# Two decode layers on one core: layer 0's output product runs one pair behind, its last two output weights load last, the MLP loads are recut, and the tile context is dropped

## The chip, the cores and the metric

The kernel runs on one core of one Trainium2 chip. The metric is the device time of one execution in microseconds (us). Six runs of the kernel before gave 523.41 to 524.87 us, with a median of 523.86 us.

## The reference

One token goes through two layers that share all their weights. Each layer is attention over a sliding window followed by a gated MLP, both with a residual:

```python
x = x + A(layernorm(x)); x = x + B(layernorm(x))      # twice, same weights and caches
# A: 32 heads of 192, the last 4096 keys and values of each head
q = (x @ wq).reshape(B, Sq, 32, 192)
p = softmax(einsum("bhqd,bhkd->bhqk", q, k) * 192**-0.5)
o = einsum("bhqk,bhkd->bhqd", p, v);  A = o.reshape(B, Sq, 32*192) @ wo
# B: 640 -> 1536 -> 640
h = sigmoid(x @ w_gate) * (x @ w_up);  B = h @ w_down
```

All is bf16. x has 640 elements. There is one query, so every weight and every cache entry is used once per layer, and 219 MB come from HBM in an execution.

## The kernel before, in words

**Units and slots.** The 32 heads are worked in 16 pairs. For each pair the host has laid out two units of 128 partitions by 14208 elements (3552 KB, KB of 1024 bytes): `ua[p]` holds the query weights (1920 elements) and then the keys, `ub[p]` holds the values (VE = 12288 elements, head after head) and then the output weights (WOE = 1920 elements). SBUF has seven slots of one unit (L132) and a region `mreg` of 12288 elements, which is 19.2 cells of FW = 640. The MLP's gate, up and down weights are 12 cells each. `A_SLOT` and `B_SLOT` (L183 to L189) say which slot a unit goes to. In layer 0 the ua units alternate between slots 0 and 1 and the ub units between slots 2 and 3, apart from a few. Units a0, a1, a14, a15, b0, b14 and b15 stay in their slots after layer 0 and are used again in layer 1 without a load (`KEPT`); in layer 1 the values of pair 1 (PM) go into `mreg`, and its output weights ("wom") into the slot of a1 once that pair's query product is done.

**Loads.** All loads are issued from SyncE (L182) in the fixed order of the list `seq` (L204 to L209): a0, a1, b0, a2, b1, a3, b2, ... a15, b14, then pair 15's second-head values with its output weights ("b1"), its first-head values in two halves ("b0"), and then the layer-0 MLP: gate cells 0 to 4 and 5 to 11 ("wg"), up cells 0 to 6 ("u1") and 7 to 11 ("u2"), down cells 0 to 6 ("d1") and 7 to 11 ("d2"), the values of pair PM in three parts ("va", "vb", "vc"). Then come layer 1's a2 in two parts ("a0"), "wom", and the pairs up to 13, and the weights of the last MLP. A load is planned as soon as the list reaches it and its place is free: `release` frees a slot, `mark` records an event, and `try_load` (L222) refuses an item whose event is not there yet. On the chip SyncE waits in this order for the semaphore of the reader that frees the place. "u2" waits for the first gate product, "d1" for both, "d2" for the first part of the up product, and "va" to "vc" for both down products.

**A step.** `step(p, prev)` (L459) computes the query product Q(p) on TensorE (L351), the scores QK(p) (L366), the maximum in `soft` (VectorE L376, ScalarE L379, TensorE L382, VectorE L383 and L385), the exponential (ScalarE L390), then for the pair before the product with the values PVmm (L420) and its copies (ScalarE L425), for p the transposed probabilities ET (L396, L400, L403, L405), and at last PVout of the pair before: six small matmuls (L435), one VectorE multiply into `oTb` (L438) and 15 matmuls with the output weights into `yT` (L445). The last of these frees the ub slot. Layer 0 runs pair 0 by hand, `step(1, 0)`, and a loop on TensorE over the steps 2 to 15, then PVmm and PVout of pair 15 and the residual (L334). Layer 1 begins with the kept pairs 14, 15, PM and 0 in an interleaved order written out by hand, and then runs the same steps.

**MLP of layer 0.** Sum, centring, the gate product in two parts and the up product in two parts (`proj`, L558), the sigmoid as Exp, add and reciprocal (L588 to L590), the product `hT` in two parts (L593), the down product in two parts (L605), the residual.

**Ends.** The kernel opens a tile context (L795) with one critical section (L113). `finish` (L610) follows the block: the last down product per load (L617), a copy (L621), the store (L623), a wait for it, and six semaphore clears (L626).

Of the kernel before, what the change touches and what calls it, by code (L numbers as in the profile page):

```python
# [44 lines left out]
class _Prog:  # L45

    def __init__(self):
        self.ops = {e: [] for e in ("pe", "dve", "act", "dma", "adma")}
        self.cnt = {e: 0 for e in ("pe", "dve", "act")}
        self.dcnt = {}  # L50
        self.seg = None
# [55 lines left out]
def decode_kernel(ctx: ExitStack, tc: tile.TileContext, cx: bass.AP, ua: bass.AP, ub: bass.AP,  # L107
                  wg_d: bass.AP, wu_d: bass.AP, wd_d: bass.AP, out: bass.AP):
    nc = tc.nc
# [3 lines left out]
    ctx.enter_context(tc.tile_critical(name="decode", no_gpsimd_drain=True))  # L113
# [24 lines left out]
    sh = sb("sh", [P, 6 * DC + 4 + FC], BF16)  # L138
# [3 lines left out]
    oTb = sh[:, 6 * DC:6 * DC + 3]  # L142
    hT = sh[:, 6 * DC + 4:6 * DC + 4 + FC]
# [26 lines left out]
    rm = {n: res("m_" + n) for n in "abc"}  # L170
    MOFF = {"a": (0, 5 * FW), "b": (5 * FW, 12 * FW), "c": (12 * FW, ME)}
# [32 lines left out]
    seq += [("wg", 0), ("wg", 1), ("u1",), ("u2",), ("d1",), ("d2",), ("va",), ("vb",), ("vc",)]  # L204
    tail = stream(1, range(2, 14))
    assert tail[0] == ("a", 1, 2)
    seq += [("a0", 0), ("a0", 1), ("wom",)] + tail[1:]
    seq += [("fg",), ("fu",), ("fd", 0), ("fd", 1), ("fd", 2)]
    seq_pos = [0]  # L209
    busy = set()  # L210
# [3 lines left out]
    GH = 5  # L214
# [10 lines left out]
    def try_load(it):  # L225
        k = it[0]
        if k in ("a", "b"):
            s = (A_SLOT if k == "a" else B_SLOT)[it[1]][it[2]]
            if not take(s):
                return False  # L230
            pg.dma(q_dma(slot(s, 0, UNIT), (ua if k == "a" else ub)[it[2]]), f"s{s}", wr=[rslot[s]])
        elif k == "b1":
            s = B_SLOT[it[1]][it[2]]
            if not take(s):
                return False
            n = len(pg.ops["dma"])
            pg.dma(q_dma(slot(s, NB * DH, UNIT - NB * DH), ub[it[2]][:, NB * DH:]), f"s{s}", wr=[rslot[s]])
            ev_done["b1"] = list(pg.ops["dma"][n]["deps"].items())
        elif k == "b0":
            s = B_SLOT[it[1]][it[2]]  # L240
            o = it[3] * NHALF
            pg.dma(q_dma(slot(s, o, NHALF), ub[it[2]][:, o:o + NHALF]), f"bh{it[3]}", wr=[res(f"bh{it[3]}")], extra=ev_done["b1"])
        elif k == "a0":
            if f"a14_{it[1]}" not in ev_done:
                return False
            s = A_SLOT[1][2]
            o0, o1 = ((0, A0CUT), (A0CUT, UNIT))[it[1]]
            pg.dma(q_dma(slot(s, o0, o1 - o0), ua[2][:, o0:o1]), f"a0{it[1]}", wr=[res(f"a0{it[1]}")] + ([rslot[s]] if it[1] else []),
                   extra=[ev_done[f"a14_{it[1]}"]])
        elif k == "wg":  # L250
            f0, f1 = ((0, GH), (GH, FC))[it[1]]
            pg.dma(q_dma(mreg(f0 * FW, (f1 - f0) * FW), wg_d[:, f0 * FW:f1 * FW]), f"wg{it[1]}", wr=[[rm["a"]], [rm["b"]]][it[1]])
        elif k == "u1":
            pg.dma(q_dma(mreg(12 * FW, 7 * FW), wu_d[:, 0:7 * FW]), "u1", wr=[rm["c"]])
        elif k == "u2":
            if "gate0" not in ev_done:
                return False
            pg.dma(q_dma(mreg(0, 5 * FW), wu_d[:, 7 * FW:]), "u2", wr=[rm["a"]])
        elif k == "d1":
            if "gate1" not in ev_done:  # L260
                return False
            pg.dma(q_dma(mreg(5 * FW, 7 * FW), wdp(0, 7)), "d1", wr=[rm["b"]], extra=[ev_done["gate0"]])
        elif k == "d2":
            if "up0" not in ev_done:
                return False
            pg.dma(q_dma(mreg(12 * FW, 5 * FW), wdp(7, 12)), "d2", wr=[rm["c"]])
        elif k in ("va", "vb", "vc"):
            if "down0" not in ev_done:
                return False
            o0, o1 = MOFF[k[1]]  # L270
            pg.dma(q_dma(mreg(o0, o1 - o0), ub[PM][:, o0:o1]), k, wr=[rm[k[1]]])
        elif k == "wom":
            if "QM" not in ev_done:
                return False
            pg.dma(q_dma(slot(A_SLOT[1][PM], 0, WOE), ub[PM][:, VE:UNIT]), "wom", wr=[res("wom")], extra=[ev_done["QM"]])
        elif k == "fg":
            pg.dma(q_dma(mreg(0, 12 * FW), wg_d), "fg", wr=[rm["a"], rm["b"], rm["c"]])
        elif k == "fu":
            if not take(U_SLOT):
                return False  # L280
            pg.dma(q_dma(slot(U_SLOT, 0, 12 * FW), wu_d), f"s{U_SLOT}", wr=[rslot[U_SLOT]])
        else:
            if it[1] == 0 and not take(D_SLOT):
                return False
            c0, c1 = WFIN[it[1]]
            pg.dma(q_dma(slot(D_SLOT, c0 * D, (c1 - c0) * D), wdp(c0, c1)), f"wf{it[1]}", wr=[rslot[D_SLOT]] if it[1] == 0 else [])
        return True
# [50 lines left out]
    def attention(l, xi):  # L338
# [6 lines left out]
        def Q(p, y):  # L345
            sa = A_SLOT[l][p]

            def f(t):
                for i, c0 in enumerate((0, P, 2 * P)):
                    for c in range(DC):  # L350
                        ins = t.matmul(qe[:, i:i + 1], lhsT=slot(sa, c * 2 * DH + c0, P), rhs=xq[:, c:c + 1], start=(c == 0), stop=(c == DC - 1))  # L351
                return ins
            ev = pg.op("pe", f, rd=[res("xq"), rslot[sa]] + ([res("a00")] if l == 1 and p == 2 else []), ex=[rb[3]])
            pg.op("dve", lambda v: v.tensor_tensor(out=qs[:, y], in0=qe[:, 0:3].unsqueeze(2).to_broadcast([P, 3, 32]), in1=mask3, op=ALU.mult),  # L354
                  rd=[res("cst")], wr=[res(f"qs{y}")], ex=[rb[3]])
            return ev
# [51 lines left out]
        def PVmm(p, z):  # L408
# [3 lines left out]
            for h in (1, 0) if half else (0, 1):  # L412
                vt = (mreg(h * NB * DH, NB * DH) if inm else slot(sv, h * NB * DH, NB * DH)).rearrange("p (t d) -> p t d", t=NB)
                for part in (0, 1) if half and h == 0 else (None,):
# [8 lines left out]
                    rV = list(rm.values()) if inm else [rslot[sv]] + ([] if part is None else [res(f"bh{part}")])  # L423
# [4 lines left out]
        def PVout(p, z):  # L428
            inm = l == 1 and p == PM
            sv = None if inm else B_SLOT[l][p]  # L430

            def tm(t):
                for c in range(3):
                    for sg in range(2):
                        ins = t.matmul(oT3[:, c:c + 1], lhsT=o8_sb[:, sg, c:2 * DH:3], rhs=mask2[:, sg:sg + 1], start=(sg == 0), stop=(sg == 1))  # L435
                return ins
            pg.op("pe", tm, rd=[res("o8sb0"), res("o8sb1"), res("cst")], ex=[rb[6]])
            pg.op("dve", lambda v: v.tensor_scalar(out=oTb, in0=oT3[:, 0:3], scalar1=Rn[z], scalar2=None, op0=ALU.mult),  # L438
                  rd=[res(f"Rn{z}0"), res(f"Rn{z}1")], wr=[res("oTb")], ex=[rb[6]])
            wo = slot(A_SLOT[1][PM], 0, WOE) if inm else slot(sv, VE, WOE)  # L440

            def im(t):
                for j in range(DC):
                    for c in range(3):
                        ins = t.matmul(yT[:, j:j + 1], lhsT=wo[:, c * D + j * P:c * D + (j + 1) * P], rhs=oTb[:, c:c + 1],  # L445
# [3 lines left out]
            pg.op("pe", im, rd=[res("oTb")] + ([res("wom"), rslot[sa]] if inm else [rslot[sv]]), ex=[rb[7]])  # L449
            if inm:  # L450
                release(sa)
            elif not (l == 0 and ("b", p) in KEPT):
                release(sv)

# [4 lines left out]
        def step(p, prev):  # L459
            Q(p, 0)  # L460
            QK(p, 0)
            soft()
            expo()
            PVmm(prev, prev % 2)
            ET(p % 2)
            PVout(prev, prev % 2)
# [14 lines left out]
        if l == 0:  # L481
# [9 lines left out]
            p = NPAIR - 1  # L491
        else:
            Q(14, 0)
            ln_sq(xi)
            mark("a14_0", QK(14, 0, ks=(0,)))
            mark("a14_1", QK(14, 0, ks=(1, 2)))
            Q(15, 1)
            ln_rstd(K2_ATT, eps_a, srs_c, res("srs"))
            mark("QM", Q(PM, 0))
            QK(15, 1, 1)  # L500
# [3 lines left out]
            Q(0, 1)  # L504
            soft(1)
            expo(1)
            QK(0, 1)
# [6 lines left out]
            QK(PM, 0)  # L514
# [10 lines left out]
            p = 13  # L525
        PVmm(p, p % 2)
        PVout(p, p % 2)
# [10 lines left out]
    def mlp(l, xi):  # L538
# [23 lines left out]
        if last:  # L562
            proj(0, range(FC), g_of, 0, [rm["a"], rm["b"], rm["c"]])
        else:
            mark("gate0", proj(0, range(GH), g_of, 0, [rm["a"]]))
            mark("gate1", proj(0, range(GH, FC), g_of, 0, [rm["b"]]))
# [9 lines left out]
        HS = (0, 7, FC)  # L576
        if last:
            u_of = lambda fb: slot(U_SLOT, fb * FW, FW)
            ru = [[rslot[U_SLOT]]] * 2
        else:  # L580
            u_of = lambda fb: mreg(12 * FW + fb * FW, FW) if fb < 7 else mreg((fb - 7) * FW, FW)
            ru = [[rm["c"]], [rm["a"]]]
        ubank = (1, 6)
        proj(ubank[0], range(0, 7), u_of, 1, ru[0])
        if not last:
            mark("up0")
        proj(ubank[1], range(7, FC), u_of, 1, ru[1], 7)
# [10 lines left out]
        for i in range(2):  # L598
            c0, c1 = HS[i], HS[i + 1]
            wd = mreg((5 if i == 0 else 12) * FW, (c1 - c0) * D)  # L600
# [7 lines left out]
            pg.op("pe", f, rd=[res(f"hT{i}"), rm["b"] if i == 0 else rm["c"]], ex=[rb[7]])  # L608
        mark("down0")
        return residual(xi)  # L610

    def finish():
# [10 lines left out]
        nc.sync.dma_start(out.rearrange("b s (g n) -> (b s g) n", g=NRG), o_row[0:32 * NRG:32]).then_inc(tail_sem["out"], 16)  # L623
        nc.sync.wait_ge(tail_sem["out"], 16)
        for t_ in tail_sem.values():
            nc.sync.sem_clear(t_)  # L626
# [90 lines left out]
    with nc.Block() as block:  # L717
# [3 lines left out]

        @block.vector
# [76 lines left out]
```

## Time and profile before

The profiled execution took 524.68 us itself, 0.82 us over the median of the six; its span on the chip is 522.9 us, and 1.8 us lie around the span.

| what | value |
|---|---|
| median of six runs, their range | 523.86 us, 523.41 to 524.87 us |
| profiled execution, its span | 524.68 us, 522.9 us |
| busy share of TensorE matmuls, weight loads, VectorE, ScalarE, GpSimd | 53%, 27%, 19%, 17%, 0% |
| HBM read, mean rate over the span | 219.18 MB, 419 GB/s |
| one full unit in the steady part, landing to landing | 8.43 us |
| granted TensorE clock, mean | 0.58 |

How to read it: a busy share is an average over the span. The page cuts the span into 40 slices of 13.07 us and gives a rate for each. A DMA is split over 16 DMA engines; the trace has a landing record for each of them, and a reader waits for the last. Where this document speaks of the first and the last engine's landing, it means these records.

### The profile page before, as it was taken

Reading aid. Unit: us, or ns where it says so; the run is one execution under the profiler, and the core shown is the slowest. Engines: PE = TensorE matmul, PEld = TensorE weight load, DVE = VectorE, ACT = ScalarE, POOL = GpSimd, SP = SyncE. Lnnn points to the kernel's source line nnn. Section 1 sums busy time; section 2 is a strip of 40 time slices with the busy share of each in tenths; the row PEclk is TensorE's granted clock in tenths of the full one; section 3 lists DMA queues with packets and bytes.
Section 4 is the critical chain, followed back from the end, with each engine's and each line's share of the span. In section 5 each row is a group of like instructions: output and inputs, shape, how many; then the busy total and the mean of one; then the engine's idle time right before and its main releaser. Section 6 shows DMA issues by size and latency. Waiting matters only on the chain.

```text
span 522.9 us, 8445 instructions
## 1 busy us (share of the span) xinstructions
PE 277.6 (53%) x3716; PEld 139.9 (27%) x3716; DVE 97.9 (19%) x372; ACT 88.0 (17%) x171; POOL 0.2 (0%) x4
## 2 busy tenths in 40 slices
PE   0545354554545354544564768767554554545365
PEld 0222122222222122222224434433222222222133
DVE  1312111112011111112011233232211112011110
ACT  0122111210122101210120033222211210122110
POOL 0000000000000000000000000000000000000000
PEclk9765666656655555555555557765766656555555
DMA  8999999999999999999999999999999999999995
GB/s 350 430 432 434 431 423 433 433 430 437 424 435 430 428 437 426 433 433 428 437 409 352 364 439 432 432 425 432 427 430 435 426 435 430 429 433 433 421 424 235
DMA packets 11115, 219.45 MB, mean 420 GB/s; under 512 B 1368, under 2 KB 1368, under 8 KB 2904
## 3 DMA queue, kind: packets, MB, share of 16 engines
q1 hardware_dynamic: 10952, 219.13, 98.3%
q8 instruction: 13, 0.21, 0.2%
q10 hardware_dynamic: 144, 0.06, 0.1%
q14 instruction: 6, 0.05, 0.0%
HBM read 219.18 MB, written 0.00 MB: 419 GB/s over the span
## 4 chain that ended last, share of the span: by engine, by line
DMA 73%; PE 18%; DVE 4%; SPq 1%; issue 1%; ACT 1%; ACTq 0%; DVEq 0%
DMA big<-in_ub_dram 61%; PE o L420 8%; DMA big<-in_wd_dram 7%; DMA big<-in_wu_dram 5%; PE scores L366 3%; PE bank L403 2%; PE bank L445 1%; SPq L182 1%; PE bank L396 1%; ACT e_sb L390 1%; DVE sc L405 1%; PE bank L382 1%; DVE et_sb L400 1%; DVE sh L438 1%; PE bank L351 1%
## 5 line engine op out<-in xcount | busy, mean ns | idle before, releaser
L420 PE MATMUL o<-big,et_sb 128*2 128x384 bf16 x1024 | 86.1, 510 | 53.1 <-DMA big<-in_ub_dram 53.1
L366 PE MATMUL scores<-big,qs 128*32 128x512 bf16 x744 | 84.7, 626 | 10.3 <-DVE qs L354 9.8
L379 ACT ACTIVATE diag<-cst,sc 128x128 f32<-128x128 bf16 x32 | 12.8, 401 | 265.2 <-DVE sc L376 251.2
L351 PE MATMUL bank<-sh,big 128*128 128x1 bf16 x480 | 17.7, 166 | 73.5 <-DMA big<-in_ua_dram 72.6
L420 PEld LDWEIGHTS o<-big,et_sb 128*2 128x2 bf16 x1024 | 29.2, 113 | 97.2 <-DMA big<-in_ub_dram 62.5
L376 DVE TENSOR_REDUCE sc<-scores 128x1 f32<-128x1024 f32 x31 | 37.9, 1223 | 81.3 <-PE scores L366 81.3
L382 PE MATMUL bank<-diag,sc 128*128 128x128 f32 x64 | 23.4, 464 | 47.6 <-ACT diag L379 47.6
L390 ACT ACTIVATE e_sb<-scores,sc 128x1024 bf16<-128x1024 f32 x31 | 37.3, 1204 | 41.4 <-DVE sc L385 39.5
L425 ACT CAST o_sb<-o 128x384 bf16<-128x384 f32 x64 | 30.6, 477 | 75.7 <-PE o L420 75.5
L366 PEld LDWEIGHTS scores<-big,qs 128*32 128x32 bf16 x744 | 24.2, 135 | 45.3 <-issue 32.7
L351 PEld LDWEIGHTS bank<-sh,big 128*128 128x128 bf16 x480 | 15.9, 106 | 76.4 <-DMA big<-in_ua_dram 74.5
L382 PEld LDWEIGHTS bank<-diag,sc 128*128 128x128 f32 x64 | 14.7, 285 | 73.2 <-ACT diag L379 71.3
L400 DVE CAST et_sb<-bank 128x64 bf16<-128x64 f32 x32 | 7.2, 224 | 126.0 <-PE bank L396 126.0
L354 DVE TENSOR_TENSOR qs<-bank,cst 128x96 bf16<-128x96 f32 x32 | 8.2, 258 | 105.6 <-PE bank L351 105.5
L445 PE MATMUL bank<-sh,big 128*128 128x1 bf16 x480 | 17.4, 165 | 16.3 <-DVE sh L438 16.3
L403 PE MATMUL bank<-sc 128*128 128x2 f32 x64 | 15.7, 315 | 14.4 <-DVE sc L401 14.4
L445 PEld LDWEIGHTS bank<-sh,big 128*128 128x128 bf16 x480 | 14.7, 100 | 18.9 <-DVE sh L438 18.4
L403 PEld LDWEIGHTS bank<-sc 128*128 128x128 f32 x64 | 13.0, 253 | 17.3 <-DVE sc L401 17.3
L383 DVE TENSOR_REDUCE sc<-bank 128x2 f32<-128x128 f32 x32 | 9.3, 291 | 42.9 <-PE bank L382 42.9
L396 PEld LDWEIGHTS bank<-cst,e_sb 128*128 128x128 bf16 x256 | 9.1, 104 | 23.2 <-ACT o_sb L425 16.7
L396 PE MATMUL bank<-cst,e_sb 128*128 128x8 bf16 x256 | 11.9, 170 | 5.7 <-ACT e_sb L390 5.7
L405 DVE RECIPROCAL sc<-bank 64x1 f32<-64x1 f32 x64 | 10.6, 166 | 19.7 <-PE bank L403 18.6
(60 smaller groups left out, 98.1 us busy)
## 6 DMA issues: line engine op xcount, KB each, us to landing
big<-in_ua_dram SPq DMA_DIRECT2D x27, 3552.0 KB, 30.0
big<-in_ub_dram SPq DMA_DIRECT2D x26, 3552.0 KB, 28.3
big<-in_ub_dram SPq DMA_DIRECT2D x2, 2016.0 KB, 16.3
big<-in_ub_dram SPq DMA_DIRECT2D x4, 768.0 KB, 18.5
big<-in_ua_dram SPq DMA_DIRECT2D x1, 2048.0 KB, 12.6
big<-in_wg_dram SPq DMA_DIRECT2D x1, 1920.0 KB, 23.3
big<-in_wu_dram SPq DMA_DIRECT2D x1, 1920.0 KB, 27.4
big<-in_ua_dram SPq DMA_DIRECT2D x1, 1504.0 KB, 8.8
```

The source lines that it names most:

```text
L351: ins = t.matmul(qe[:, i:i + 1], lhsT=slot(sa, c * 2 * DH + c0, P), rhs=xq[:, c:c + 1], start=(c == 0), stop=(c == DC - 1))
L366: ins = t.matmul(sc_x[1 + b][32 * j:32 * j + 32, :], lhsT=qs[:, y, k, :], rhs=slot(sa, WQE + k * W + (4 * b + j) * 512, 512), start=(k == ...
L376: pg.op("dve", lambda v: v.reduce_max(out=mx, in_=sc_x[0][:], axis=AX.X), wr=[res("mx")], ex=sc_x[3:5])
L379: pg.op("act", lambda a: a.mul(out=diag[:], in_=ident, mul=mx), rd=[res("cst"), res("mx")], wr=[res("diag")])
L382: pg.op("pe", lambda t: t.matmul(dmx[:, 0:P], lhsT=ones_f, rhs=diag[:], start=True, stop=True), rd=[res("diag"), res("ones")], ex=[rb[2]])
L390: pg.op("act", lambda a: a.activation(out=e_sb[:], in_=sc_x[0][:], func=ACT.Exp, bias=nbias, scale=srs_c, accum_out=rowsum), rd=[res("nbia ...
L396: ins = t.matmul(qe[:, 0:2 * NB].rearrange("p (r x) -> p r x", r=2)[:, :, 4 * b:4 * b + 4], lhsT=e_sb[:, b * P:(b + 1) * P], rhs=sel, star ...
L403: pg.op("pe", lambda t: t.matmul(dmx[:, P:P + 2], lhsT=ones_f, rhs=rs2, start=True, stop=True), rd=[res("rs2"), res("ones")], ex=[rb[2]])
L405: pg.op("dve", lambda v, h=h: v.reciprocal(out=Rn[z][64 * h:64 * h + 64], in_=dmx[64 * h:64 * h + 64, P + h:P + h + 1]), wr=[res(f"Rn{z}{h ...
L420: ins = t.matmul(o8[h][32 * j:32 * j + 2, 0:2 * DH].rearrange("p (a d) -> p a d", a=2), lhsT=et_sb[:, z, h * NB + 2 * u:h * NB + 2 * u + 2 ...
L425: pg.op("act", lambda a, h=h: a.copy(out=o8_sb[:, :, h * DH:(h + 1) * DH], in_=o8[h][:, 0:2 * DH].rearrange("p (a d) -> p a d", a=2)), wr= ...
L445: ins = t.matmul(yT[:, j:j + 1], lhsT=wo[:, c * D + j * P:c * D + (j + 1) * P], rhs=oTb[:, c:c + 1], start=False, stop=(c == 2), skip_grou ...
```

## The change

In layer 0 `PVout` is split. `PVt` (the six small matmuls and the multiply) stays in its step; `PVn` (the 15 matmuls with the output weights, and the release of the ub slot) moves to the next step, behind `soft` and ahead of `expo` and of the next `PVmm`. `oTb` gets two buffers. Behind the loop PVn(14) and PVn(15) come last. For this b0 and b14 load their values alone. The output weights of pair 0 are loaded into slot 2 right behind b0, and GpSimd copies them to slot 5 after PVn(0), since layer 1 uses them from there; b2 waits for that copy. The output weights of pairs 14 and 15 ("wol", 480 KB each) load behind the last values.

The MLP weights are cut in other places, and each load waits for the cells that it overwrites: gate 0 to 5 and 6 to 11 (cells 0 to 11 of the region), up 0 to 4 (cells 12 to 16), 5 to 6 (17 to 18) and 7 to 11 (cells 0 to 4, after the first gate part), down 0 to 5 (cells 5 to 10, after both gate parts) and 6 to 11 (cells 11 to 16, after the second gate part and the first up part). The values of PM come in four parts: cells 0 to 4 after the last up part, 17 to 19 after the second, 5 to 10 and 11 to 16 after the first and the second down part. The load "wom" moves ahead of the two parts of a2, and the query product of PM moves ahead of the scores of pair 14, into bank 6 and the second `qs` buffer; pairs 15 and 0 take the first. The tile context and its critical section go; the five other semaphores are cleared before the wait for the store instead of behind it.

```diff
-decode_kernel(ctx: ExitStack, tc: tile.TileContext, ...
-    ctx.enter_context(tc.tile_critical(name="decode", no_gpsimd_drain=True))
+decode_kernel(ctx: ExitStack, nc, ...
...
-    MOFF = {"a": (0, 5 * FW), "b": (5 * FW, 12 * FW), "c": (12 * FW, ME)}
+    MW = {"wg0": (0, 0, 6), "wg1": (6, 6, 12), "u1": (12, 0, 5), "u2": (17, 5, 7), "u3": (0, 7, 12), "d0": (5, 0, 6), "d1": (11, 6, 12)}
+    MAFTER = {"u3": ("gate0",), "d0": ("gate0", "gate1"), "d1": ("gate1", "up0")}
+    MV = {"v0": (0, 5), "v1": (17, len(rc)), "v2": (5, 11), "v3": (11, 17)}
+    VAFTER = {"v0": "up2", "v1": "up1", "v2": "down0", "v3": "down1"}
...
     seq = stream(0, range(NPAIR))
-    seq += [("wg", 0), ("wg", 1), ("u1",), ("u2",), ("d1",), ("d2",), ("va",), ("vb",), ("vc",)]
+    seq.insert(seq.index(("b", 0, 0)) + 1, ("wo0",))
+    seq += [("wol", 14), ("wol", 15)] + [(k,) for k in (*MW, *MV)]
...
-    seq += [("a0", 0), ("a0", 1), ("wom",)] + tail[1:]
+    seq += [("wom",), ("a0", 0), ("a0", 1)] + tail[1:]
...
-    busy = set()
+    busy = {2}
...
+        def PVn(p, z):
+            inm = l == 1 and p == PM
+            sv = None if inm else 2 if l == 0 and p == 0 else B_SLOT[l][p]
...
+            if l == 0 and p == 0:
+                pg.op("pool", lambda g: g.tensor_copy(out=slot(5, VE, WOE), in_=slot(2, VE, WOE)), rd=[rslot[2]], wr=[res("wol0")])
+                release(2)
...
             QK(p, 0)
             soft()
+            if l == 0 and prev > 0:
+                PVn(prev - 1, 1 - prev % 2)
             expo()
             PVmm(prev, prev % 2)
             ET(p % 2)
-            PVout(prev, prev % 2)
+            PVt(prev % 2)
+            if l == 1:
+                PVn(prev, prev % 2)
...
             p = NPAIR - 1
+            PVmm(p, 1)
+            PVt(1)
+            PVn(p - 1, 0)
+            PVn(p, 1)
         else:
             Q(14, 0)
+            mark("QM", Q(PM, 1, 6))
             ln_sq(xi)
             mark("a14_0", QK(14, 0, ks=(0,)))
             mark("a14_1", QK(14, 0, ks=(1, 2)))
-            Q(15, 1)
+            Q(15, 0)
             ln_rstd(K2_ATT, eps_a, srs_c, res("srs"))
-            mark("QM", Q(PM, 0))
-            QK(15, 1, 1)
+            QK(15, 0, 1)
...
         nc.sync.dma_start(out.rearrange("b s (g n) -> (b s g) n", g=NRG), o_row[0:32 * NRG:32]).then_inc(tail_sem["out"], 16)
+        for k in tail_sem:
+            if k != "out":
+                nc.sync.sem_clear(tail_sem[k])
         nc.sync.wait_ge(tail_sem["out"], 16)
-        for t_ in tail_sem.values():
-            nc.sync.sem_clear(t_)
+        nc.sync.sem_clear(tail_sem["out"])
...
-    with _tile.TileContext(nc) as tc:
-        decode_kernel(tc, *args, o)
+    decode_kernel(nc, *args, o)
```

## The prediction

> **What bounds the kernel now.** I read the page first: rates, queues, chain.
>
> ```profile
> span 522.9 us, 8445 instructions
> ...
> GB/s 350 430 432 434 431 423 433 433 430 437 424 435 430 428 437 426 433 433 428 437 409 352 364 439 432 432 425 432 427 430 435 426 435 430 429 433 433 421 424 235
> ...
> q1 hardware_dynamic: 10952, 219.13, 98.3%
> ...
> DMA 73%; PE 18%; DVE 4%; SPq 1%; issue 1%; ACT 1%; ACTq 0%; DVEq 0%
> ```
>
> The load queue takes 98.3% of the 16 DMA engines' time, and the rate stands near 432 GB/s in all slices but the first, the last and numbers 21 to 23 (261 to 301 us): the change from layer 0 through its MLP to layer 1. 219.13 MB at 432 GB/s are 507 us, so 16 us of the span can be had at all. The bytes do not change. So I look only for time in which the DMA engines have nothing queued, and for the ends. The windows of 2 us around the MLP show the first (columns: stretch, length, busy time of PE, PEld, DVE, ACT, POOL, clock, DMA share, GB/s):
>
> ```profile
> 278.00:280.00 2.00, 1.39 (x34) 1.25 (x30) 0.70 (x8) 0.00 (x0) 0.00 (x0) 0.50 0.98 412
> 280.00:282.00 2.00, 1.71 (x45) 1.54 (x41) 0.00 (x0) 0.19 (x1) 0.00 (x0) 0.50 0.64 181
> ...
> 292.00:294.00 2.00, 1.20 (x20) 0.98 (x17) 0.64 (x6) 0.00 (x0) 0.00 (x0) 0.50 0.83 335
> 294.00:296.00 2.00, 1.83 (x20) 0.90 (x24) 0.26 (x4) 0.00 (x0) 0.00 (x0) 0.50 0.93 315
> ```
>
> The cause is in SyncE's own timeline (start, time to the end of the last issue of the group, load):
>
> ```profile
> 238.62 18.15 SPq L182 DMA_DIRECT2D big<-in_ub_dram  x4
> ...
> 257.77 22.78 SPq L182 DMA_DIRECT2D big<-in_wu_dram  x2
> 281.37 3.01 SPq L182 DMA_DIRECT2D big<-in_wd_dram  x2
> 287.07 5.35 SPq L182 DMA_DIRECT2D big<-in_ub_dram  x3
> ```
>
> "u2" is issued at 280.2 (the end of the second line, less 0.33), when the gate has read its cells; the queue is nearly empty then. It happens again when "vb" waits for the down product. The landing records put numbers on it. On the last engine, landing to landing: u2 3.26 us where 800 KB at the steady rate (3552 KB in 8.43) are 1.90, d1 3.09 for 2.66, vb 4.22 for 2.66, vc 3.06 for 2.73: **3.7 us of gaps**. On the first engine the same intervals, with those of d2 and a2, exceed the rate by 4.6 us.
>
> The engines do not run level: b14 lands at 264.5 on the first and 266.9 on the last, and the final load at 516.6 and 518.9. The spread begins in the first 70 us, where 16 KB instruction pages, about 1 us each, ride on single engines; they do so again in layer 1.
>
> **The change part by part.**
>
> *Tile context, start.* The barrier ends at 0.66, then a tile NOP and a branch, and the first load is issued at 0.95. Without the two: **-0.2**.
>
> *End.* SyncE has the store's completion at 521.49, clears six semaphores until 521.84, and the tile exit (two barriers, a range clear) runs to 522.87. After, one clear is left: 5 x 0.06 + 1.0 = **-1.3**. The 1.8 us around the span I leave as they are. If another closing barrier takes the exit's place, 0.4 to 1.0 of it comes back.
>
> *MLP loads.* From the last value half's landing (call it x) the queue holds 960 KB of wol, 1920 KB of gate, 1120 KB of up: 9.5 us at 2.37 us per 1000 KB. Before, bh1 landed at 275.55 and the gate began at 279.38, 3.8 behind. Now PVn(15) needs wol15 (x+2.3), so the gate begins near x+4.3, but waits for its cells at x+4.6; it ends near x+5.7 (30 matmuls, 60 took 1.96). u3 is issued 4 us ahead of the queue's end. Then come d0 (issued after gate1 at x+8.0, with the last engine busy until x+11.6), and in the same way d1 (x+9.8, x+14.0), v0 and v1 (x+12.6, x+16.3), v2 (x+15.0, x+19.1), v3 (x+17.3, x+21.4), wom (x+19.6, x+23.8), a2 (x+20.5, x+24.9). Each is 3 us or more early, where an empty queue needs 1.0 us from issue to the first packet (u2 280.22 to 281.18, vb 290.43 to 291.40) and about 2.1 until the last engine moves. So **the old gaps go: -3.7 on the last engine, -4.6 on the first**. Five loads more than before cost 0.04 each (wg0, wg1 and u1 take 7.35 for 7.22 at the steady rate): **+0.2**.
>
> *Output product a pair behind.* It takes nothing off TensorE: the same 15 matmuls (0.56) in another place, under the wait for the next values. What moves is the release of the ub slot. Step 15 of the profile gives the new time:
>
> ```profile
> 258.56 0.56 PE L351 MATMUL bank<-sh,big 128*128 128x1 bf16 x15 [3.09 <-DMA big<-in_ua_dram]
> 259.46 2.75 PE L366 MATMUL scores<-big,qs 128*32 128x512 bf16 x24 [0.35 <-DVE qs L354]
> 263.98 0.80 PE L382 MATMUL bank<-diag,sc 128*128 128x128 f32 x2 [1.76 <-ACT diag L379]
> ```
>
> The keys land, and 6.2 us on the last matmul of `soft` ends; PVn adds 0.56. So b(p+1) is issued 6.8 us after a(p+1) lands; before, it was issued some 5 us after b(p-1) landed, about 10 us earlier. In the steady part b(p) and a(p+2) are still to land then, 16.9 - 6.8 = 10 us: covered, even for engines 2.4 ahead. **At the end of layer 0 it is not**: no a16 follows. Behind a15 there is only b14, now values alone (3072 KB, 7.29), and SyncE's order lets nothing pass pair 15's values. These were issued from 255.5 on, behind PVn(13) of step 14; now from 265.4 on (264.78 + 0.56). The last engine would be done with b14 at 266.5 - 1.14 = 265.35, the first at 264.05 - 1.14 = 262.9. First packets come from 266.3 to 267.5. **New gap: +1.0 to +2.1 on the last engine, +3.4 to +4.5 on the first.**
>
> *Sum of the queue.* Last engine: -3.7 + 1.5 + 0.2 = -2.0. First: -4.6 + 3.9 + 0.2 = -0.5. The end is that of the worst of sixteen. After the new gap they start level, but instruction pages then hit others than the one that is last today; so I choose between: **-1.3**, bounds -0.4 and -2.6.
>
> *The copy on GpSimd* (128x1920 bf16, once) has no row; its four memsets (0.1) carry no rate. VectorE's maximum over 1024 elements takes 1.22 (1.2 ns each), L354 0.26 for 96 (2.7 ns): 2.3 to 5.2 us, and the nearest by shape is 2.3. It starts at 45 (a2 lands at 38.4, + 6.8). b2 waits for it, with a4 behind it on SyncE; a3 keeps the first engine busy to 53.2, the last to 55.5, so less 1.0 for issue the cover is 7 to 9 us: nothing. A VectorE operation on two SBUF inputs (L385, 0.16 to 0.24) lies beside it. The Trainium skill, "SBUF — State Buffer", section "Who interferes with whom", speaks against the copy: such an operation and a GpSimd one that reads SBUF exclude each other for the whole instruction. No run here has shown it. By it L385 could be late by the whole copy, in step 2 alone, where 10 us of queue lie ahead: the sum would be the same.
>
> *Layer 1.* Compute starts there when down1 is done, x+17.3; x is 274.5, so 291.8 for 292.0 before. The queue arrives about 2 us earlier. Its tightest place is pair 2's values, issued at 311.02 with the queue full to 319.2: 8.2 us become 6, enough. Moving Q(PM) shifts 0.5 us of matmul into the wait for `qs` (0.35): nothing, and if not, 0.2 under the same cover. The last MLP is untouched.
>
> **Sum**: 524.68 - 0.2 - 1.3 - 1.3 = 521.9 for the profiled execution. That is 0.82 over the median, so on the median **521.1**.
>
> **Rivals.**
> 1. *The new gap eats all.* The early engines become the last ones (first-engine sum, or two pages on one of them), so only the ends gain. For it: a spread of 2.3 came back within layer 1 today. 523.86 - 1.5 = 522.4 (521.9 to 522.8).
> 2. *The middle goes whole.* The gap at b15 stays within the last engine's lag and no page falls on it: -1.5 - 2.6 to -3.7, so 519.4 (518.6 to 520.2). Against it: 265.4 is later than 265.35 already.
> 3. *It doesn't do what it says.* A closing barrier stays, and the gaps only move: within 0.2% of 523.86, 522.8 to 524.9.
> 4. *Slower*: the copy on GpSimd. Past 7 to 9 us, each further us holds b2, and a4 behind it, by one. To turn -2.8 into +1.05 it must take about 12 us, 6 ns an element, over twice the slowest row. 526.
>
> **How the numbers follow.** Forecast (520.2 to 521.9) 0.48, rival 1 0.20, rival 2 0.17, rival 3 0.10, rival 4 0.05. The range takes in the forecast, rival 1 and most of rival 2: 519.1 to 522.9. A measurement here tells 0.2%, 1.05 us, from no change; faster by that means under 522.8: 0.48 + 0.20 + 0.17 = 0.85, less a little for rival 1's upper edge: 0.84. Within: 0.11. Slower: 0.05.
>
> **What would show it.** The rate should be near 420 GB/s without a dip from 276 to 300, and a new dip of 2 to 3 us should stand just before 267, with SyncE waiting for L445's release at about 265. The gate's first load should land before the gate could start. The span should end 0.2 us behind the store's completion. GpSimd's copy should end by 50, and VectorE L385 of step 2 may be late. Wrong would be: a dip near 53 us (the copy), a dip that stays at 280 or 290 (the recut), or a later last landing than 518.7.

## The result, and the profile after

The changed kernel takes 523.26 us (median of 35 runs, 522.17 to 524.41); the kernel before takes 524.44 in 76 runs (the first six had given 523.86). The ratio is 0.9976, 95% interval 0.9970 to 0.9983: **1.2 us less, between 0.9 and 1.6**. The forecast was 2.8 less. The profiled execution took 523.98 us itself, its span is 522.7.

The page after, the lines that answer to those shown of before:

```profile
span 522.7 us, 8408 instructions
...
GB/s 353 440 427 432 429 426 439 426 432 428 431 437 425 437 426 431 437 426 435 432 288 418 385 442 434 427 432 423 432 435 429 431 428 433 435 431 428 421 426 267
...
q1 hardware_dynamic: 11672, 219.13, 98.4%
...
DMA 70%; PE 19%; DVE 5%; SPq 2%; ACT 2%; issue 1%; another core or an unknown queue 1%; ACTq 0%; DVEq 0%
```

The loss has changed its place. Slices 21, 22 and 23 had 409, 352 and 364 GB/s; now they have 288, 418 and 385. The windows (stretch, length, busy time of PE, PEld, DVE, ACT, POOL, clock, DMA share, GB/s) show why:

```profile
262.00:264.00 2.00, 0.48 (x8) 0.00 (x0) 1.23 (x1) 0.21 (x1) 0.00 (x0) 0.50 0.49 209
264.00:266.00 2.00, 1.18 (x17) 1.03 (x17) 0.46 (x3) 0.58 (x2) 0.00 (x0) 0.50 0.03 12
266.00:268.00 2.00, 1.91 (x28) 0.84 (x32) 0.00 (x0) 1.32 (x3) 0.00 (x0) 0.50 0.78 203
...
280.00:282.00 2.00, 0.96 (x30) 0.88 (x30) 0.00 (x0) 0.00 (x0) 0.00 (x0) 0.50 1.00 413
...
292.00:294.00 2.00, 0.72 (x27) 0.72 (x28) 0.00 (x0) 0.00 (x0) 0.00 (x0) 0.50 0.99 401
294.00:296.00 2.00, 1.48 (x36) 1.31 (x33) 0.45 (x5) 0.00 (x0) 0.00 (x0) 0.50 1.05 424
```

The stretches at 280, 292 and 294, which had 181, 335 and 315 GB/s, are full. The new hole stands at 263 to 267. SyncE and TensorE in step 15 (start, time, operation) show its cause:

```profile
258.82 0.56 PE L351 MATMUL bank<-sh,big 128*128 128x1 bf16 x15 [4.21 <-DMA big<-in_ua_dram]
...
264.25 0.80 PE L382 MATMUL bank<-diag,sc 128*128 128x128 f32 x2 [1.76 <-ACT diag L379]
264.84 0.58 PE L450 MATMUL bank<-sh,big 128*128 128x1 bf16 x15
```

```profile
265.45 2.31 SPq L182 DMA_DIRECT2D big<-in_ub_dram  x5
267.80 0.99 SPq L182 DMA_DIRECT2D big<-in_wg_dram  x2
268.84 12.55 SPq L182 DMA_DIRECT2D big<-in_wu_dram  x3
```

PVn(13) (L450) frees the slot at 265.42, and only then SyncE issues pair 15's values and everything behind them. The landing records give the size; in each cell the last engine's landing stands first, the first engine's second:

| landed, us | before | after | after, second profile |
|---|---|---|---|
| a15 | 258.51, 256.08 | 258.77, 256.00 | 258.09, 255.88 |
| b14 | 266.95, 264.52 | 266.04, 263.29 | 265.36, 263.17 |
| pair 15's second-head values | 271.79, 269.33 | 271.52, 271.01 | 271.02, 270.29 |
| a2 and wom | 310.78, 308.47 | 311.19, 309.17 | 309.65, 308.64 |
| last load | 518.92, 516.60 | 520.09, 517.44 | 519.16, 516.66 |
| end of the span | 522.90 | 522.67 | 521.75 |

The second-head values are 3.65 us of queue (1536 KB). They land 5.48 after b14 on the last engine and 7.73 on the first, so the hole is **1.8 us on the last engine and 4.1 on the first**. In the end the last load does not land earlier than before. What the change gains inside the span is behind it: 2.6 us from there to the end, where 4.0 were. The execution less its span is 1.3 us, where it was 1.8.

### The profile page after: what moved, and what is told of

It reads as the page before. It is cut to its first block, busy times and chain, and to the rows that moved or that the text cites. A ratio compares the mean times of both kernels' runs of the same rounds, so it can differ in the third digit from the quotient of the medians.

```text
span 522.7 us, 8408 instructions
## 1 busy us (share of the span) xinstructions
PE 272.1 (52%) x3716; PEld 139.3 (27%) x3716; DVE 99.4 (19%) x372; ACT 87.7 (17%) x171; POOL 2.0 (0%) x5
## 4 chain that ended last, share of the span: by engine, by line
DMA 70%; PE 19%; DVE 5%; SPq 2%; ACT 2%; issue 1%; another core or an unknown queue 1%; ACTq 0%; DVEq 0%
DMA big<-in_ua_dram 31%; DMA big<-in_ub_dram 28%; DMA big<-in_wd_dram 8%; PE scores L366 7%; PE o L420 5%; DMA big<-in_wu_dram 3%; DVE sc L376 2%; SPq L182 2%; PE bank L382 2%; PE bank L450 1%; PE bank L351 1%; PE bank L403 1%; ACT e_sb L390 1%; ACT diag L379 1%
## 5 line engine op out<-in xcount | busy, mean ns | idle before, releaser
L351 PEld LDWEIGHTS bank<-sh,big 128*128 128x128 bf16 x480 | 15.7, 105 | 87.6 <-DMA big<-in_ua_dram 85.6
L450 PE MATMUL bank<-sh,big 128*128 128x1 bf16 x480 | 17.8, 166 | 7.9 <-DVE sh L439 7.6
L450 PEld LDWEIGHTS bank<-sh,big 128*128 128x128 bf16 x480 | 17.1, 103 | 10.0 <-DVE sh L439 8.4
```

## The experiments

All ratios are to the kernel before, run beside each kernel on the same chip; the time ahead of a ratio is a median. The kernels ran in three groups on three chips: the first from the anchor to the first run of the ends alone, the second with PVn ahead of Q, the release later still, the pair with the old loads and the first instruction pages, the third the rest. Between groups the ratios are compared. Two theories stood against each other. Theory 1: the hole behind b14 gives back what the recut gains. Theory 2: what happens in the middle does not reach the end.

**The anchor**, no edit.

> The changed kernel once more, as the anchor for the other runs on this chip. Both theories expect 1.0 to 1.5 us less than the kernel before. What it also tells is whether its instruction pages fall on the same DMA engines in a second profile: if the last landing of up cells 7 to 11 again comes 1.4 us late on the last engine alone, and the spread at the last load is again 2.6, they do.

522.71 us, ratio 0.9969 (0.9956 to 0.9982). Up cells 7 to 11 ("u3") took 3.17 us on the last engine and 1.96 on the first, with a spread of 1.9 behind them where 0.7 was ahead. At the last load the spread is 2.5. As in the first profile it is one engine of the sixteen that falls behind at u3 (1.93 behind the first, the next 0.72; 1.98 and 0.50 in the first profile), while an instruction page is fetched (at 285.64). Here it does not seem to be the engine that had been last, for one still stands 0.72 behind the first as the last one did before (0.73).

**Filling the hole.**

```diff
+    seq.insert(seq.index(("b1", 0, 15)), ("wg0",))
-    seq += [("wol", 14), ("wol", 15)] + [(k,) for k in (*MW, *MV)]
+    seq += [("wol", 14), ("wol", 15)] + [(k,) for k in (*MW, *MV) if k != "wg0"]
```

> The changed kernel with one load moved: the first gate part (960 KB, 2.28 us of queue, its place is free) is issued between b14 and pair 15's values. Theory 1 (the hole behind b14, 1.8 us on the last engine and 4.1 on the first, gives back what the recut gains): the hole is filled on the last engine and halved on the first, 1.2 to 2.3 us less than the changed kernel. Theory 2 (the last engine is made anew by instruction pages, and what happens in the middle does not reach the end): within 0.4 us of the changed kernel.

520.92 us, ratio 0.9937 (0.9915 to 0.9960), 1.8 less than the anchor. Pair 15's values are issued at 265.1 as before, but the last engine has a gap of 0.06 in place of 2.0, the first one of 1.4 in place of 3.5. Theory 2 falls.

**The recut without the pair behind.** The edit puts `PVn(prev)` back behind `PVt` in every step, loads b0, b14 and b15 whole, and drops wo0, wol and the copy.

```diff
-            if l == 0 and prev > 0:
-                PVn(prev - 1, 1 - prev % 2)
...
-            if l == 1:
-                PVn(prev, prev % 2)
+            PVn(prev, prev % 2)
```

> The changed kernel without its first part: the output product stands in its old place in all steps, pair 15's and 14's output weights load with their values, no copy on GpSimd; the recut MLP loads, the moved query product of PM and the missing tile context stay. Theory 1: no hole behind b14, so 1.5 us for the ends and 1.6 to 3.5 for the recut, 3.1 to 5.0 less than the kernel before. Theory 2: the ends alone, 1.3 to 1.8 less than before, like the changed kernel.

520.76 us, ratio 0.9931 (0.9907 to 0.9955): 3.4 less than before and 1.95 less than the anchor. So the pair behind costs 1.95 where the recut is in place. The result lies in theory 1's range, at its lower end.

**The ends alone.** Twice, since the first interval was wide. Besides the lines shown, five semaphores are cleared ahead of the wait for the store, as in the change.

```diff
-    ctx.enter_context(tc.tile_critical(name="decode", no_gpsimd_drain=True))
...
-    with _tile.TileContext(nc) as tc:
-        decode_kernel(tc, *args, o)
+    decode_kernel(nc, *args, o)
```

> The kernel before without the tile context and with five semaphores cleared ahead of the wait for the store; nothing else. Both theories: 1.3 (end) to 1.5 (with the start) less than before. If the changed kernel's own start (first load and constants asked for within 6 ns of each other, a0 0.2 us later on the last engine) belongs to the missing context, 1.0 to 1.3.

> The kernel before without the tile context once more, for a narrower interval: 1.5 to 2.5 less than the kernel before.

522.11 us, ratio 0.9946 (0.9926 to 0.9966), and 522.75 us, ratio 0.9970 (0.9953 to 0.9987): 1.4 to 2.1 less by the medians (1.6 to 2.8 by the ratios), more than the 1.5 of the forecast on average. The traces have the reason outside the span: the execution less its span is 1.78 us before and 1.3 to 1.4 in all profiles without tile context. With 1.4 at the end and 0.2 at the start that makes 2.0 to 2.1.

With the ends alone at 1.4 to 2.1 and the whole change at 1.2, **the middle as a whole gains nothing, and may lose some tenths**. The recut alone gains 1.35 more than the ends by the medians of the first group (0.8 by the ratios), and the pair behind takes it back.

With theory 2 gone another rival was to be told from theory 1, called 2' in what follows: that the split itself costs the time, by its 15 matmuls in a new place or by the late output weights.

**The release early, the pair still behind.** Two lines move, within the step.

```diff
         def step(p, prev):
+            if l == 0 and prev > 0:
+                PVn(prev - 1, 1 - prev % 2)
             Q(p, 0)
             QK(p, 0)
             soft()
-            if l == 0 and prev > 0:
-                PVn(prev - 1, 1 - prev % 2)
             expo()
```

> The changed kernel with two lines moved: PVn of two pairs back stands ahead of Q(p) in its step, in place of behind soft(p). It still runs a pair behind and pairs 14's and 15's output weights still load last, but the slot is released when it was before the change. Theory 1 (the release is what costs): no hole behind b14, pair 15's values issued near 255.5, 1.5 to 3.0 us less than the changed kernel and 3.0 to 4.5 less than the kernel before. Theory 2' (the split itself, the 15 matmuls or the late output weights cost it): like the changed kernel, within 0.5.

520.42 us, ratio 0.9920 (0.9902 to 0.9938): 4.0 less than before and **the lowest median here**. The windows at the same place:

```profile
262.00:264.00 2.00, 0.23 (x5) 0.21 (x2) 1.22 (x1) 0.40 (x1) 0.00 (x0) 0.50 0.97 412
264.00:266.00 2.00, 0.92 (x10) 0.45 (x14) 0.46 (x3) 0.85 (x1) 0.00 (x0) 0.50 0.99 418
266.00:268.00 2.00, 2.00 (x32) 0.76 (x24) 0.00 (x0) 0.93 (x3) 0.00 (x0) 0.50 0.95 396
```

The hole is gone with the same matmuls and the same late output weights, and the kernel is 2.6 to 2.9 us faster than the changed one and its anchor by the ratios. It was the time of the release, not the split. Against the kernel with the recut alone (0.9931) the late output weights and the pair behind are worth 0.6, which these intervals cannot tell from nothing.

**The release later still.**

```diff
             expo()
             PVmm(prev, prev % 2)
+            if l == 0 and prev > 0:
+                PVn(prev - 1, 1 - prev % 2)
             ET(p % 2)
```

> The changed kernel with PVn of two pairs back another place later, behind PVmm of the pair before: its end moves from 265.4 to about 269.3 in step 15, 3.9 us later, all else as it is. Theory 1: the queue is already empty there, so each further us is paid in full by every DMA engine: 3.9 us more than the changed kernel (3.4 to 4.4), and the hole grows from 1.8 to 5.7 us on the last engine. The other steps have 10 us of cover and pay nothing. Theory 2': no change within 0.5.

527.76 us, ratio 1.0061 (1.0040 to 1.0082), 4.5 more than the changed kernel by the ratios. The windows of this kernel:

```profile
264.00:266.00 2.00, 0.58 (x2) 0.50 (x2) 0.93 (x1) 0.40 (x1) 0.00 (x0) 0.50 0.58 246
266.00:268.00 2.00, 0.94 (x13) 0.37 (x16) 0.46 (x3) 1.22 (x2) 0.00 (x0) 0.50 0.00 0
268.00:270.00 2.00, 2.00 (x30) 0.63 (x22) 0.00 (x0) 0.56 (x2) 0.00 (x0) 0.50 0.00 0
270.00:272.00 2.00, 1.46 (x33) 1.29 (x31) 0.54 (x4) 0.48 (x1) 0.00 (x0) 0.50 0.43 80
```

The hole on the last engine is 5.5 in place of 1.8. SyncE issues pair 15's values 3.3 us behind b14's landing there (270.52 and 267.23), where it was 0.6 ahead (265.45 and 266.04): 3.9 us later, and the hole is 3.7 longer. The rest stands ahead of it, and the expectation that the other steps pay nothing was wrong: b14 lands at 267.23 on the last engine, where it landed at 266.04 and 265.36. In those steps PVmm waits for b(p-1), which lands 8.4 us behind a(p), so the release comes not 3.9 but some 5 us later, and the first engine's landings show extra waits of 0.2 to 0.7 us in five units.

**The pair behind with the old MLP loads.** The edit restores the old cuts of gate, up, down and PM's values, and the old place of Q(PM) and wom.

```diff
+    MW = {"wg0": (0, 0, 5), "wg1": (5, 5, 12), "u1": (12, 0, 7), "u2": (0, 7, 12), "d0": (5, 0, 7), "d1": (12, 7, 12)}
+    MAFTER = {"u2": ("gate0",), "d0": ("gate0", "gate1"), "d1": ("up0",)}
+    MV = {"v0": (0, 5), "v1": (5, 12), "v2": (12, len(rc))}
+    VAFTER = {"v0": "down1", "v1": "down1", "v2": "down1"}
```

> The changed kernel with the old MLP loads: gate, up, down and PM's values cut as before the change, wom behind the two parts of a2, the query product of PM in its old place; the output product a pair behind, the late output weights and the missing tile context stay. If the parts add up, the pair costs 1.9 over the kernel without tile context (the changed kernel against the one with the recut alone): 0 to 0.5 less than the kernel before. If the hole only eats time that the old gaps would have cost anyway (the engines start level behind it), less than that: 0.5 to 1.2 less than before.

523.68 us, ratio 0.9986 (0.9973 to 0.9998). Against the ends alone (0.9946 and 0.9970) the pair costs 0.8 to 2.1. The times neither show nor exclude that the hole eats part of the old gaps. The landings of this one profile speak for it: on the last engine the old loads take 34.2 us behind the hole, and 34.9 to 35.4 without one (the table further down).

**Instruction pages.** GpSimd has nothing to do, so waits that are already satisfied can be put on it; they only lengthen its program.

```diff
         def _(g):
             emit("pool", g)
+            for _ in range(2048):
+                g.wait_ge(S["pool"], 1)
```

> The kernel with PVn ahead of Q (label e6_front) and 2048 waits that are already satisfied, on GpSimd behind its one copy, so eight more instruction pages of 16 KB (256 instructions each) have to be fetched between 30 and 150 us, where the load queue is full; nothing waits for GpSimd there. If a page costs time at the end when it falls on the engine that is last: 0.6 us for each such page, 0.6 to 2.5 more than that kernel, and the spread of the landings grows in steps of 0.4 to 1.1 at the pages. If pages are hidden, as the instruction counts alone would say: the same within 0.4, and the spread stays at 2.5.

523.98 us, ratio 0.9986 (0.9971 to 1.0000): **3.6 us more than the same kernel without them**, also more than the 2.5 put down as the most, in a stretch where nothing waits for GpSimd. The line of the page for that instruction queue, first of the kernel with PVn ahead of Q, then of this one (packets, MB, share of the 16 engines' span):

```profile
q14 instruction: 6, 0.05, 0.0%
```

```profile
q14 instruction: 14, 0.11, 0.1%
```

Eight more packets, of 8 KB each and not 16, cost 0.7% of the time. The landing records say where. The first three new pages cost the last engine nothing. With each of the other five, fetched from 75.5 to 121.4 us, the unit then in flight lands later on it, by 0.24, 0.66, 0.85, 0.66 and 0.65 us over the 8.43 of the steady part. The spread goes from 2.6 to 5.6 and stays there until the MLP. That the fetches are what delays these units is read from their standing together.

**The same pages ahead of the hole**: the edit above in the changed kernel.

> The changed kernel itself with the same 2048 satisfied waits on GpSimd between 30 and 120 us (eight more instruction pages). In the kernel without the hole they cost 3.6 us. If the hole and the lag of the last engine overlap (the hole holds up the leading engines by 4 us and lets the last one catch up, so a lag built before it is partly free): 0.8 to 2.0 more than the changed kernel, and the last engine's gap at pair 15's values goes from 1.8 to under 0.5. If they add up: 3.0 to 4.0 more, and the gap stays at 1.8.

526.90 us, ratio 1.0049 (1.0035 to 1.0064), 3.8 to 4.2 more than the changed kernel and its anchor by the ratios. The gap on the last engine stays at 1.8, and on the first it is 6.9. My idea that the hole lets the last engine catch up falls: TensorE waits for the last engine's part of a15, which lands 2.9 us later than in the changed kernel (261.67 and 258.77), and pair 15's values are issued 2.9 us later (268.34 and 265.45). The end of the hole moves with the last engine. **Lag and hole add up.**

**Four pages in the MLP's stretch**, in the kernel with the ends alone and in the one with PVn ahead of Q: 1024 waits on GpSimd for a count of TensorE's that is reached at step 15. The first of the two needs a block for GpSimd.

```diff
+            for _ in range(1024):
+                g.wait_ge(S["pe"], pg.pool_at)
```

> The kernel without tile context, with the old MLP loads and the old order, and 1024 satisfied waits on GpSimd from step 15 on (250 to 305 us): four more instruction pages in the stretch where this kernel has gaps in its load queue. If pages in a gap are free, which would be why filling the gaps gave less than the gaps were long: 0 to 0.9 more than the same kernel without them. If not: 1.5 to 2.5 more.

> The same four pages in the same stretch of the kernel with PVn ahead of Q, whose queue has no gap there: 1.3 to 2.8 more than the same kernel without them in either case. If it is under 0.9, pages fall on other engines here and say nothing on the gaps.

522.29 us, ratio 0.9960 (0.9945 to 0.9975), and 520.77 us, ratio 0.9928 (0.9913 to 0.9944): no cost in either that the intervals (0.8 us to each side) can tell. By what was expected of the second, the pair says nothing on whether gaps hide pages. Four pages of GpSimd do not delay the last engine at 264 and 275, where the queue is full. It fits that GpSimd's pages all fall on one DMA engine, which starts some 2 us ahead of the last: the first three or four are free, and each further one costs 0.65 us. The packets do not name their engine, so that is argued, not shown.

## Why the prediction was right or wrong

**The bound: right.** With a hole of 5.5 us on the last engine the kernel took 527.76 us, with 1.8 us 523.26, and with none 520.42.

**The hole: right in place, cause and size.** It was forecast from step 15's own lines at 1.0 to 2.1 us on the last engine and 3.4 to 4.5 on the first; it is 1.8 and 4.1 (2.0 and 3.5 in the second profile), and the release is at 265.4 as worked out. One move of two lines removes it, and 2.6 to 2.9 us with it.

**"The old gaps go: -3.7 on the last engine, -4.6 on the first": the step that failed.** The gaps do go for the most part, but the last engine gains only a third to a half of it. From the landing of the last load ahead of the gate to that of a2 and wom, the same 12864 KB (30.5 us at the steady rate) took on the last engine

| | old MLP loads, us | recut, us |
|---|---|---|
| without the hole | before 35.2; ends alone 35.1, 35.4; with four pages 34.9 | without the pair 33.6; PVn ahead of Q 33.9; with four pages 32.9; with eight 32.8 |
| behind the hole | pair with the old loads 34.2 | changed kernel 33.5, 32.5; release later still 33.4; with eight pages 33.1 |

On the mean of these profiles the recut gains **1.9 without the hole and 1.1 behind it, in place of 3.5** (3.7 less the 0.2 for more loads). 2.7 us above the steady rate remain on the mean. Some 0.05 for each of 14 loads explains 0.7. In the changed kernel the rest stands where instruction pages are fetched: one at 286.07, and u3 lands 3.43 us behind u2 on the last engine and 1.96 on the first, though it was issued 3.6 us before u2 had landed on the first; one at 308.65, and a2's second part takes 5.50 where 4.86 are due. The pages are of 16 KB and by their pace TensorE's: 249 matmuls and weight loads start between the fetches at 286.07 and 296.65. The prediction named pages for the first 70 us and for layer 1, but put their cost in the MLP's stretch at nothing. Nor were its 3.7 us all gap. In the kernel before, one engine of the sixteen lands vb 0.95 behind the next, where a page is fetched at 294.99; an empty queue would hold up all of them. That the page did it is argued, since the records name no engine. Whether the old gaps hid pages was tried and stays open. With the recut alone a gap for the leading engines also stays at u3, 3.38 us for 1.90 on the first engine; there the values and not the output weights land last.

**"The end is that of the worst of sixteen ... -1.3, bounds -0.4 and -2.6": outside its bounds.** The last load landed 1.2 later than before in one profile and 0.2 in the other, at 520.09 and 519.16; a last landing later than 518.7 was put down as a sign of being wrong. -1.1 for the recut behind the hole and +1.8 to 2.0 for the hole make +0.7 to +0.9. The two profiles part at units in flight when a page was fetched. Rival 1, given 0.20, had this outcome, that only the ends gain; its range of 521.9 to 522.8 on the first six runs was still below the 523.26 measured.

**The ends: right in the span, too small outside.** The tail behind the last landing shrank by 1.4 (forecast 1.3). The first load is issued at 0.74 instead of 0.95, as forecast, but the constants' load is then issued 6 ns from it, and in the two profiles of the changed kernel a0 lands 0.15 earlier and 0.2 later on the last engine. The 1.8 us around the span, which I left as they are, became 1.3 to 1.4. That the ends gave more than forecast hid a part of what the middle lost: the time was nearer to the forecast than the mechanism.

**The copy on GpSimd: no cost, as forecast**, though not at the time put down. It starts at 30 and not at 45, ahead of PVn(0): it reads what PVn(0) only reads too, so it waits for the load alone. VectorE's L385 stands beside it:

```profile
30.06 1.78 POOL L460 COPY big<-big 128x1920 bf16<-128x1920 bf16 x1 [29.62 <-DMA big<-in_ub_dram]
30.09 1.76 DVE L385 CUSTOM_DVE_ANT_0 sc<-sc 128x2 f32<-128x2 f32 x1
```

The copy's 1.78 us is less than the 2.3 taken. L385, which reads two inputs from SBUF, takes 0.16 us in its other 31 places. Here it starts 0.03 behind the copy and ends with it: it is late by the whole copy, in step 1 and not in step 2. This agrees with the rule on shared ports that the prediction cites. In the other eight profiles with the copy this instruction was over before the copy began. In one of them (the changed kernel with eight pages) another VectorE instruction, L401, began 1.06 us behind the copy's start and took 0.75 us in place of 0.22, also to the copy's end. As the prediction said, the delay costs nothing: the next query product waits for a2, at 38.47.

**Layer 1: covered, as forecast.** Behind a2 the units land 8.43 apart on the first engine until the last MLP, with one exception of 0.3.

**The sum**: forecast -1.5 for the ends and -1.3 for the middle; measured about -1.4 to -2.1 and +0.2 to +0.9. The forecast was set on a base of 523.86 from six runs; 76 runs put it at 524.44, which moves the forecast by 0.6, to 521.7. The rest of the miss, 1.6 us or more, is the middle's.

## What to carry to other kernels

When work is postponed, look for what it releases, and follow the load queue to the last item behind it: a cover of 10 us in every step of a loop was 0 in the one step that had no next unit. Where the same shift can be had with the release in its old place (here: first in the next step, not in its middle), take that. And in a queue that is full, do not take every late landing for a gap: an empty queue held up all sixteen engines here, and what delays one alone stays when the gap is closed.

## What the runs showed of the hardware that was not expected

Instructions that do nothing can cost time in a kernel bound by loads. 2048 satisfied waits on an idle GpSimd cost 3.6 us (and 3.8 to 4.2 in the changed kernel). Eight more pages are fetched for them, and loads in flight at the last five land 0.24 to 0.85 us late on the last engine. 1024 of them in another stretch cost nothing that could be told (522.29 against 522.11 and 522.75, 520.77 against 520.42). The records fit that a page costs time when it falls on the engine that is last or makes one the last; they do not name the engine. TensorE's pages of 16 KB seem to do the same, 1.5 us on one engine at u3 in the changed kernel. The spread of the landings at the last load lay between 2.1 and 4.6 us in the profiles, and the profile with 4.6 was of an execution of 524.46 us, the slowest of its seven.

A VectorE instruction of 0.16 us with two inputs in SBUF took 1.76 us beside a GpSimd copy that had started 0.03 us ahead of it, and ended with the copy.

Dropping the tile context took 0.4 to 0.5 us outside the span as well, 1.78 to between 1.3 and 1.4.
